# Subtracting the softmax maxima of four attention units on TensorE, and placing three pieces of work elsewhere, in a windowed attention followed by a SoLU block

## The chip, the core and the metric

The kernel runs on one core of a Trainium2 chip. The metric is the device time of one execution in microseconds. Before the change it is 503.84 us, the median of three runs (502.17 to 504.85). The core has five engines with a sequencer each: TensorE (PE in the profile, with its weight loads as PEld), VectorE (DVE), ScalarE (ACT), GpSimd (POOL) and SyncE (SP), which here issues the DMA transfers. They run side by side and wait for one another by semaphores. Matmuls write to PSUM, which this kernel sees as eight banks of 512 fp32 columns (`banks[:, 0:8]`).

## What is computed

Attention over 8 batches, 8 heads, 576 positions and 64 dimensions, in which a position sees only the 32 before it (heads 0 to 3) or every fourth of the 128 before it (heads 4 to 7). Its output, 4608 tokens of 512, goes through a block with the SoLU activation and a layer norm:

```python
scores = scale * np.matmul(q, k.transpose(0, 1, 3, 2))
scores = np.where(masks[None, :, :, :], scores, -1000000000.0)
scores = scores - np.max(scores, axis=-1, keepdims=True)
attn = np.exp(scores)
attn = attn / (np.sum(attn, axis=-1, keepdims=True) + 1e-09)
attn_out = np.matmul(attn, v)
...
h = x @ w_in                                   # 4608 x 512 by 512 x 1024
sm = e / (np.sum(e, axis=-1, keepdims=True) + 1e-09)   # e = exp(h - max)
solu = h * sm
ln = (solu - mu) / np.sqrt(var + 1e-06) * g_ln
out = ln @ w_out                               # 1024 x 512
```

## The kernel before

**Units.** A unit is two heads of one batch; there are 32. For unit n, SyncE loads queries and keys (`qN`) and values (`vN`). TensorE computes the scores of a unit (`SN`, function `scores`): two bf16 matmuls write the mask into PSUM (L244, an identity times the mask), and 80 small fp32 matmuls add the scores (L252; `order` prints x40 for a shape, the trace counts each fp32 matmul twice, as it does its weight load). The result is 128 partitions by 2 x 5 x 64: for every query 64 keys. Then come `maxN` (VectorE, L278, maximum over 64 keys, ten per partition), `subN` (the maximum is subtracted), `expN` (ScalarE, L295), `sumN` and `invN` (VectorE, L299 to L304), `normN` (GpSimd, L309), `turnN` (a transpose on VectorE, L314) and `VN` (TensorE, probabilities by values, L330). `xhN` and `xlN` split the output into two fp32r parts, which are the columns of x.

For units 0 to 9 the mask is written by TensorE, and `subN` is a VectorE operation from PSUM to SBUF (L288); for units 2, 5 and 6 ScalarE copies the scores first (`cpN`) and GpSimd subtracts (L291).

**PSUM.** `ps_s(n)` gives the scores of units 0 to 4 the banks 2 and 3, and all later units a part of banks 6 and 7. The output of `VN` has banks of its own (`ps_x`). The block's first product of even and odd tiles lies in pairs of banks too: hc1 of the opening, the second half of tile 1, starts in a pair that the scores used.

**The block.** 36 tiles of 128 tokens. `haI`, `hbI`, `hcI`, `hdI` are the four quarters of the first product (L398, 6 matmuls each, fp32r by three terms: hi x hi, hi x lo, lo x hi), then `peakI` (VectorE, L409), `eI` (ScalarE), `gateI` and `midI` (VectorE, L433, L441), `varI` (GpSimd), `forthI` and `backI` (the tile goes out to a scratch array in DRAM and comes back with the 1024 features in another order), `trAI`, `trBI` (VectorE transposes, L505), `thAI` to `tlBI` (split in hi and lo), and `oI`, the second product (L528, 24 matmuls: for each of eight groups of 128 features hi x hi, hi x lo, lo x hi), `outI`.

**Weights.** They come as 64-bit floats in 16 pieces (`wB`, 0 to 7 of w_in, 8 to 15 of w_out) and are turned to fp32 by bit operations: `absB`, `lowB` (ScalarE, L805, L815), `clampB`, `signB`, `joinB` (VectorE, L821, L828, L836), `gainB` and `hiB` (ScalarE), `loB` (GpSimd, and for some pieces, 13 among them, VectorE, L850). A product waits for the pieces that it reads: group f of `oI` for piece 8 + f.

**What sets the order.** Nothing is scheduled: each engine runs its instructions in the order in which the program issues them. For the first units and tiles that order is a list of words, `OPENING`, run from left to right; after it `STEP` and `PAIR` repeat for the rest, unchanged here. So a word moved in the list is moved on each engine that it has instructions on, SyncE's queue of DMA issues among them.

Of the kernel before, what the change touches and what calls it, by code (L numbers as in the profile page):

```python
# [9 lines left out]
F32 = mybir.dt.float32  # L10
# [4 lines left out]
AF = mybir.ActivationFunctionType  # L15
# [8 lines left out]
P = 128  # L24
# [4 lines left out]
WQ = 2 * WIN  # L29
NG = P // WIN  # L30
GQ = S // NG
NS = -(-GQ // WIN)
# [15 lines left out]
F64_MAX = REBIAS * float(np.array(0x47EFFFFF, np.uint32).view(np.float32))  # L48
FIRST = 6
OPENING = (  # L50
# [25 lines left out]
)  # L76
STEP = (
    (
# [45 lines left out]
OFFSET = {'qt2': 48, 'kt2': 32, 'vt2': 48, 'qt3': 48, 'kt3': 48, 'vt3': 48}  # L124
SLOTS = "t0 t1 t2 t3 raw4 raw5 tp t0 t1 t2 t3 raw4 raw5 tp t3 tp".split()
MERGED = 5
SHIFT = {}


@with_exitstack  # L130
def windowed_attention_then_solu_kernel(
# [10 lines left out]
    nc = tc.nc  # L142
# [6 lines left out]
    const = ctx.enter_context(tc.tile_pool(name="const", bufs=1))  # L149
    units = ctx.enter_context(tc.tile_pool(name="units", bufs=3))  # L150
    att = ctx.enter_context(tc.tile_pool(name="att", bufs=1))
# [9 lines left out]
    id_bf = packed[:, 0 : P // 2].bitcast(BF16)  # L161
    mask_sb = packed[:, P // 2 : P // 2 + NS * WQ].bitcast(BF16).rearrange("p (d c) -> p d c", d=2)
    g_sb = packed[:, P // 2 + NS * WQ :]
    mhalf = const.tile([P, 1], F32, name="mhalf")
    below = const.tile([P, 1], F32, name="below")
    w_i = const.tile([P, KT, 2, 2, 512], F32R, name="w_i")
# [3 lines left out]
    banks = psum.tile([P, 8, 512], F32, name="banks")  # L170
# [10 lines left out]

    def ps_s(n):
        if n < MERGED:
            return banks[:, 2:4, 0 : NS * WQ]
        return banks[:, 6:8, GQ : GQ + NS * WQ]

    nc.vector.memset(mhalf, -0.5)
# [45 lines left out]
    st = {}  # L233

    def scores(n):

        qt, kt = loaded[n]["q"], loaded[n]["k"]
        dil = int(n % NPAIR >= NPAIR // 2)
        ps = ps_s(n)
        st[n] = {"ps": ps.rearrange("p h (s w) -> p h s w", w=WQ)}  # L240
        on_pe = n in PE_MASK
        if on_pe:
            for h in range(2):
                nc.tensor.matmul(  # L244
                    out=ps[:, h, :], lhsT=id_bf, rhs=mask_sb[:, dil, :],
                    start=True, stop=False, skip_group_check=True,
                )
        for i in range(NS):
            for h in range(2):
                for c in range(NG):  # L250
                    q0 = GQ * c + WIN * i
                    nc.tensor.matmul(  # L252
                        out=ps[WIN * c : WIN * c + WIN, h, WQ * i : WQ * i + WQ],
                        lhsT=qt[D * h : D * h + D, q0 : q0 + WIN],
                        rhs=kt[D * h : D * h + D, q0 : q0 + WQ],
                        start=not on_pe,
                        stop=True,
                        skip_group_check=True,
                    )

    def soft_mask(n):
        if n in PE_MASK:
            return
        dil = int(n % NPAIR >= NPAIR // 2)
        sm = st[n]["sm"] = att.tile([P, 2, NS, WQ], F32, name=f"sm{n % 2}")
        nc.vector.tensor_tensor(  # L266
            out=sm.rearrange("p h s w -> p h (s w)"), in0=ps_s(n),
            in1=mask_sb[:, dil, :].unsqueeze(1).broadcast_to([P, 2, NS * WQ]),
            op=ALU.add,
        )  # L270

    def wide(x):
        return x.unsqueeze(3).broadcast_to([P, 2, NS, WQ])
# [9 lines left out]

    def soft_sub(n):
        mx = st[n]["mx"]
        if n in PE_MASK and n not in ACT_SCORES:
            sm = st[n]["sm"] = att.tile([P, 2, NS, WQ], F32, name=f"sm{n % 2}")
            nc.vector.tensor_tensor(out=sm, in0=st[n]["ps"], in1=wide(mx), op=ALU.subtract)  # L288
            return
        eng = nc.gpsimd if POOL_SUB else nc.vector  # L290
        eng.tensor_tensor(out=st[n]["sm"], in0=st[n]["sm"], in1=wide(mx), op=ALU.subtract)  # L291

    def soft_exp(n):
        sm = st[n]["sm"]
        nc.scalar.activation(out=sm, in_=sm, func=AF.Exp, scale=0.125)  # L295

# [174 lines left out]
    def part_of_t(name, i):  # L471
        name = f"{name}{i % TH_BUFS}"
        if name in SHIFT and name not in shifted:
            shifted.add(name)
            moe.tile([P, SHIFT[name]], F32, name=f"before_{name}", bufs=1)
        return moe.tile([P, FT, P], F32R, name=name, bufs=1)
# [371 lines left out]
    def conv_lo(b):  # L848
# [5 lines left out]

    one = {
        "q": load_qk, "v": load_v, "w": load_w,
        "pack": lambda _: nc.sync.dma_start(out=packed, in_=pack),
        "abs": conv_abs, "low": conv_low, "clamp": conv_clamp, "sign": conv_sign,
        "join": conv_join, "gain": conv_gain, "hi": conv_hi, "lo": conv_lo,
        "S": scores, "mask": soft_mask, "max": soft_max, "cp": soft_copy, "sub": soft_sub, "exp": soft_exp,  # L860
        "sum": soft_sum, "inv": soft_inv, "norm": soft_norm, "turn": turn,
        "V": attend, "xc": x_copy, "xh": spread_hi, "xl": spread_lo,
# [47 lines left out]
    for word in OPENING.split():  # L910
        name = word.rstrip("0123456789")
# [86 lines left out]
```

## Time and profile before

| | |
|---|---|
| median of three runs | 503.84 us |
| the profiled execution | 503.07 us, span 501.3 us |
| TensorE busy | 471.7 us, 94% of the span |
| VectorE, ScalarE, GpSimd busy | 351.9, 289.1, 295.7 us |
| DMA | 94.07 MB, mean 188 GB/s |
| subtraction of a unit on VectorE (L288) | 0.82 us |
| subtraction of a unit on GpSimd (L291) | 1.26 us |

The page cuts the span into 40 slices of 12.5 us and gives the busy share of each engine in tenths. In a timeline row stand the start, the length, the engine, the line, the operation with output and inputs by their names, how many instructions were joined in the row, and in brackets how long the engine had been idle and what released it. "issue" stands for a wait that nothing in the profile explains. In the view by stretches each row is a stretch of time with the busy time and count of TensorE, weight loads, VectorE, ScalarE and GpSimd, then the granted TensorE clock (1.00 is full), the DMA share and GB/s.

### The profile page before, as it was taken

The numbers are of one execution on the slowest core, as the hardware profiler recorded it, in microseconds if no ns is written. First come the engines' busy times: TensorE is split into PE (matmuls) and PEld (weight loads), VectorE is DVE, ScalarE is ACT, GpSimd is POOL, SyncE is SP. The second block draws the span as 40 slices with busy tenths as digits, with TensorE's granted clock in tenths as the row PEclk, the third lists the DMA queues.
The fourth block names the chain that finished last, engine by engine and source line by source line (L and its number), as shares of the span: only waits on it lengthen the run. The fifth ranks groups of instructions, "written<-read, shape, count | busy, mean of one in ns | idle before, by whom it ended". The sixth has DMA issues, their size and how long they took to land.

```text
span 501.3 us, 16598 instructions
## 1 busy us (share of the span) xinstructions
PE 471.7 (94%) x7088; PEld 379.3 (76%) x7088; DVE 351.9 (70%) x619; ACT 289.1 (58%) x481; POOL 295.7 (59%) x367
## 2 busy tenths in 40 slices
PE   3449988999999999999999999999999999999997
PEld 2337766888887888878778787878787888888876
DVE  3998897768446788787868686868676864445562
ACT  3756986645233445444457575757575767666552
POOL 0463774575344665778976666665757555766440
PEclk9999997999999999999999999999999999999999
DMA  8999637554347555565667677776765545454461
GB/s 283 349 377 346 190 78 252 150 177 154 112 130 226 179 174 162 171 194 169 200 170 221 199 218 205 214 209 211 212 211 164 161 129 147 104 157 141 109 181 70
DMA packets 50905, 94.07 MB, mean 188 GB/s; under 512 B 5648, under 2 KB 25616, under 8 KB 50832
## 3 DMA queue, kind: packets, MB, share of 16 engines
q1 hardware_dynamic: 49968, 92.30, 59.8%
q8 instruction: 55, 0.90, 0.7%
q10 hardware_dynamic: 864, 0.72, 0.4%
q14 instruction: 18, 0.15, 0.1%
HBM read 59.97 MB, written 28.31 MB: 176 GB/s over the span
## 4 chain that ended last, share of the span: by engine, by line
PE 87%; DVE 8%; DMA 2%; issue 2%; ACT 1%; SPq 0%; DVEq 0%; ACTq 0%
PE banks L528 37%; PE banks L758 20%; PE banks L398 17%; PE banks L330 6%; PE banks L252 6%; DMA t<-w_in 1%; PE banks L549 1%; DVE mag L821 1%; DVE mag L836 1%; DVE t L433 1%; DVE mx L278 1%; DVE rs L299 1%; DVE low L828 1%; DMA mid<-t 1%; PE banks L244 0%
## 5 line engine op out<-in xcount | busy, mean ns | idle before, releaser
L528 PE MATMUL banks<-w_o,th 128*128 128x512 f32 x560 | 174.9, 393 | 0.0
L528 PEld LDWEIGHTS banks<-w_o,th 128*128 128x128 f32 x560 | 103.6, 188 | 21.8 <-ACT th L513 0.4
L519 POOL TENSOR_TENSOR tl<-t,th 128x512 fp32r<-128x512 f32 x68 | 88.1, 1310 | 48.4 <-ACT th L513 48.1
L528 PE MATMUL banks<-w_o,tl 128*128 128x512 f32 x280 | 109.3, 390 | 0.0
L398 PE MATMUL banks<-w_i,x_hi 128*128 128x512 f32 x256 | 84.0, 410 | 0.1
L528 PEld LDWEIGHTS banks<-w_o,tl 128*128 128x128 f32 x280 | 52.5, 188 | 11.6 <-DVE tl L519 0.4
L513 ACT CAST th<-t 128x512 fp32r<-128x512 f32 x72 | 43.5, 620 | 28.3 <-DVE t L505 14.6
L398 PEld LDWEIGHTS banks<-w_i,x_hi 128*128 128x128 f32 x256 | 48.3, 195 | 11.1 <-DVE mu L433 0.2
L505 DVE STREAM_TRANSPOSE t<-raw 128x512 f32<-128x512 f32 x72 | 47.4, 687 | 10.4 <-DMA raw<-mid 10.3
L398 PE MATMUL banks<-w_i,x_lo 128*128 128x512 f32 x128 | 51.3, 401 | 0.0
L330 PEld LDWEIGHTS banks<-pt,vt 32*64 32x64 f32 x2816 | 35.2, 137 | 20.9 <-issue 10.5
L449 ACT ACTIVATE e<-t 128x1024 f32<-128x1024 f32 x35 | 37.0, 1057 | 21.4 <-DVE t L445 21.0
L330 PE MATMUL banks<-pt,vt 32*64 32x64 f32 (+3 forms) x2816 | 38.7, 234 | 9.9 <-DMA vt<-vw 4.0
L291 POOL TENSOR_TENSOR sm<-sm,mx 128x640 f32<-128x640 f32 x25 | 31.6, 1263 | 24.2 <-DVE mx L278 17.0
L266 DVE TENSOR_TENSOR sm<-banks,packed 128x640 f32<-128x640 f32 x22 | 18.1, 823 | 38.8 <-PE banks L252 38.8
L295 ACT ACTIVATE sm<-sm 128x640 f32<-128x640 f32 x32 | 23.6, 738 | 35.0 <-POOL sm L291 32.4
L252 PEld LDWEIGHTS banks<-kt,qt 64*32 64x32 f32 x2560 | 29.9, 113 | 16.1 <-issue 9.8
L540 ACT ACTIVATE ob<-banks,rstd 128x512 f32<-128x512 f32 x35 | 24.0, 686 | 27.9 <-issue 16.7
L252 PE MATMUL banks<-kt,qt 64*32 64x64 f32 x2560 | 35.7, 241 | 4.0 <-DMA qt<-qT 3.2
L782 DVE CUSTOM_DVE_ANT_0 t<-banks,t 128x512 f32<-128x512 f32 x30 | 20.7, 690 | 22.4 <-PE banks L758 17.0
L776 ACT COPY t<-banks 128x512 f32<-128x512 f32 x30 | 17.6, 588 | 30.3 <-PE banks L758 30.3
L442 ACT ACTIVATE t<-t,mu 128x1024 f32<-128x1024 f32 x23 | 26.4, 1149 | 11.0 <-DVE mu L441 11.0
(156 smaller groups left out, 880.0 us busy)
## 6 DMA issues: line engine op xcount, KB each, us to landing
mid<-t SPq DMA_DIRECT2D x140, 128.0 KB, 2.4
raw<-mid SPq DMA_DIRECT2D x34, 512.0 KB, 3.8
vt<-vw SPq DMA_DIRECT2D x32, 384.0 KB, 3.9
kt<-kT SPq DMA_DIRECT2D x32, 312.0 KB, 4.0
qt<-qT SPq DMA_DIRECT2D x32, 296.0 KB, 4.3
out<-ob SPq DMA_DIRECT2D x35, 256.0 KB, 2.6
x_hi<-x SPq DMA_DIRECT2D x12, 288.0 KB, 3.6
t<-w_in SPq DMA_DIRECT2D x5, 512.0 KB, 8.4
```

The costliest lines, as they stand in the source:

```text
L252: nc.tensor.matmul(out=ps[WIN * c : WIN * c + WIN, h, WQ * i : WQ * i + WQ], lhsT=qt[D * h : D * h + D, q0 : q0 + WIN], rhs=kt[D * h : D * ...
L291: eng.tensor_tensor(out=st[n]["sm"], in0=st[n]["sm"], in1=wide(mx), op=ALU.subtract)
L330: nc.tensor.matmul(out=ps_x[D * h : D * h + D, c, c0 : c0 + k1 - k0], lhsT=vt[WIN * c : WIN * c + WIN, i, D * h : D * h + D], rhs=pt[WIN * ...
L398: nc.tensor.matmul(out=ps_h(i)[:, half], lhsT=a[:, kt, xs], rhs=w_i[:, kt, half, part, :], start=(kt == 0 and k == 0), stop=(kt == KT - 1 ...
L442: nc.scalar.activation(out=dst, in_=src, func=AF.Identity, bias=mu, scale=1.0)
L449: nc.scalar.activation(out=e, in_=t, func=AF.Square, accum_out=per_tile(i, "sq"))
L505: nc.vector.transpose(out=turned(i)[:, cut(c)].rearrange("p k (a r) -> p k a r", r=WIN), in_=ms[i]["mv"].rearrange("p (a k s) -> p k a s", ...
L513: nc.scalar.copy(out=ms[i]["th"][:, cut(c)], in_=turned(i)[:, cut(c)])
L519: eng.tensor_tensor(out=ms[i]["tl"][:, cut(c)], in0=turned(i)[:, cut(c)], in1=ms[i]["th"][:, cut(c)].bitcast(F32), op=ALU.subtract,)
L528: nc.tensor.matmul(out=ps_o(i), lhsT=a[:, f, :], rhs=w_o[:, f, part, :], start=(f == 0 and k == 0), stop=(f == FT - 1 and k == 2), skip_gr ...
L540: nc.scalar.activation(out=ob, in_=ps_o(i), func=AF.Copy, scale=rstd)
L758: nc.tensor.matmul(out=banks[:, bank], lhsT=left(pa, kt), rhs=right(pb, kt), start=j in (1, 2, 5) and kt == 0 and k == 0, stop=kt == 1 and ...
```

## The change

Four things, all in the opening.

1. **Subtraction on TensorE for units 0, 1, 3 and 4** (`PE_SUB`). A new word `neg` makes a negated fp32 identity `minus` (128 x 128) on ScalarE. `soft_sub` issues two fp32 matmuls of 320 columns instead of the VectorE operation: `minus` times the maxima, broadcast over the 64 keys, is added to the scores where they lie in PSUM. `soft_exp` of these units reads PSUM and writes SBUF.
2. **PSUM of units 0 to 4.** Even units stay in banks 2 and 3, odd units go to banks 0 and 1.
3. **Values of unit 1.** `v1` is issued ahead of three weight loads rather than behind them.
4. **Unit 8.** `S8` goes from behind hb4, next to S9, to between V6 and V7; `max8` and `sub8`, still on VectorE, go from behind the transposes of tile 0 to behind `mid3`.

```diff
 OPENING = (
-    "pack q0 S0 w0 q1 max0 sub0 low0 abs0 w3 exp0 abs3 S1 q2 clamp0 low3 sign0 sum0 w2 inv0 "
+    "pack q0 S0 neg w0 q1 max0 sub0 low0 abs0 w3 exp0 abs3 S1 q2 clamp0 low3 sign0 sum0 w2 inv0 "
...
-    "norm1 turn0 S2 max2 low2 cp2 clamp1 sign2 V0 q3 turn1 sub2 clamp2 abs4 sign1 w10 hi3 low4 "
-    "w9 exp2 low7 join2 w5 join1 v1 xh0 clamp4 sign4 hi1 S3 w6 lo1 abs5 low5 sum2 inv2 xl0 max3 "
+    "norm1 turn0 S2 max2 low2 cp2 clamp1 sign2 V0 q3 turn1 sub2 clamp2 abs4 sign1 v1 w10 hi3 "
+    "low4 w9 exp2 low7 join2 w5 join1 xh0 clamp4 sign4 hi1 S3 w6 lo1 abs5 low5 sum2 inv2 xl0 "
...
+PE_SUB = (0, 1, 3, 4)
...
+    minus = const.tile([P, P], F32, name="minus")
...
         if n < MERGED:
-            return banks[:, 2:4, 0 : NS * WQ]
+            b = n % 2 * 2
+            return banks[:, 2 - b : 4 - b, 0 : NS * WQ]
         return banks[:, 6:8, GQ : GQ + NS * WQ]
...
     def soft_sub(n):
         mx = st[n]["mx"]
+        if n in PE_SUB:
+            for h in range(2):
+                nc.tensor.matmul(
+                    out=ps_s(n)[:, h, :],
+                    lhsT=minus,
+                    rhs=mx[:, h, :].unsqueeze(2).broadcast_to([P, NS, WQ]),
+                    start=False, stop=True, skip_group_check=True,
+                )
+            return
...
     def soft_exp(n):
+        if n in PE_SUB:
+            sm = st[n]["sm"] = att.tile([P, 2, NS, WQ], F32, name=f"sm{n % 2}")
+            nc.scalar.activation(out=sm, in_=st[n]["ps"], func=AF.Exp, scale=0.125)
+            return
...
+        "neg": lambda _: nc.scalar.activation(out=minus, in_=id_bf, func=AF.Copy, scale=-1.0),
```

How the instructions stand on the engines, at three places. On TensorE, around unit 4 and the first product of the block; before (L252 scores of unit 4, L330 values of unit 2, L398 first product):

```order
L252 MATMUL banks<-kt_499,qt_498 32x64 x40
L330 MATMUL banks<-pt_510,vt_489 64x64 x24
L330 MATMUL banks<-pt_510,vt_489 64x48 x8
L330 MATMUL banks<-pt_510,vt_489 64x16 x8
L398 MATMUL banks<-w_i,x_hi 128x512 x2
L398 MATMUL banks<-w_i,x_lo 128x512
```

and now, where the lines are 3 to 16 higher (L255, L346, L414) and L291 is the subtraction of unit 4:

```order
L255 MATMUL banks<-kt_503,qt_502 32x64 x40
L346 MATMUL banks<-pt_515,vt_493 64x64 x24
L346 MATMUL banks<-pt_515,vt_493 64x48 x8
L346 MATMUL banks<-pt_515,vt_493 64x16 x8
L414 MATMUL banks<-w_i,x_hi 128x512 x2
L414 MATMUL banks<-w_i,x_lo 128x512
L414 MATMUL banks<-w_i,x_hi 128x512 x2
L414 MATMUL banks<-w_i,x_lo 128x512
L291 MATMUL banks<-mx,minus 128x320 x2
```

The subtraction of unit 4 stands behind the six matmuls of ha0, ahead of hc1. That of unit 3 stands further up, between V1 and the masks of unit 4.

On TensorE, further on, values of units 6 and 7 now (they stood next to one another before):

```order
L346 MATMUL banks<-pt_1167,vt_739 64x64 x24
L346 MATMUL banks<-pt_1167,vt_739 64x48 x8
L346 MATMUL banks<-pt_1167,vt_739 64x16 x8
L247 LDWEIGHTS packed
L247 MATMUL banks<-packed 128x320
L247 LDWEIGHTS packed
L247 MATMUL banks<-packed 128x320
L255 MATMUL banks<-kt_742,qt_741 32x64 x40
L346 MATMUL banks<-pt_1181,vt_745 64x64 x24
```

The mask and scores of unit 8 (L247, L255) came in between.

On VectorE, at the same place, now (L449 gate3, L457 mid3, L281 and L300 maximum and subtraction of unit 8, L852 join11, L521 trA0, L401 xl7):

```order
L449 ISA t_1283,mu<-banks,e 128x1024
L449 ISA mu 128x1
L837 TENSOR_SCALAR mag_749<-mag_749 128x512
L457 TENSOR_SCALAR mu<-mu 128x1
L281 TENSOR_REDUCE mx<-banks 128x10
L300 TENSOR_TENSOR sm_1335<-banks,mx 128x640
L852 SCALAR_TENSOR_TENSOR mag_749<-mag_749,low_758 128x512
L521 STREAM_TRANSPOSE t_890<-raw_1165 128x512
L837 TENSOR_SCALAR mag_1327<-mag_1327 128x512
L401 TENSOR_TENSOR x_lo<-banks,x_hi 128x576
```

Before, the two operations of unit 8 stood behind the maximum of tile 4 (L409, peak4) and ahead of gate4:

```order
L409 TENSOR_REDUCE nmax<-banks 128x1
L278 TENSOR_REDUCE mx<-banks 128x10
L288 TENSOR_TENSOR sm_1400<-banks,mx 128x640
L433 ISA t_1405,mu<-banks,e 128x1024
L433 ISA mu 128x1
```

So nine operations of VectorE, from join11 to peak4, are now behind them, xl7 and the last sign of the weights among them.

42 rows, old and new, of the table OPENING are left out of this document.

## The prediction

> **What bounds the kernel now.** I read the page first, for the slices and the clock, then busy time by stage, then the timeline of single engines where TensorE waits.
>
> ```profile
> span 501.3 us, 16598 instructions
> ...
> PE 471.7 (94%) x7088; PEld 379.3 (76%) x7088; DVE 351.9 (70%) x619; ACT 289.1 (58%) x481; POOL 295.7 (59%) x367
> ...
> PE   3449988999999999999999999999999999999997
> ...
> DVE  3998897768446788787868686868676864445562
> ```
>
> ```profile
> 0.00:38.30 38.30, 16.25 (x683) 12.04 (x683) 29.46 (x51) 20.78 (x33) 14.59 (x15) 1.00 0.94 337
> 38.30:95.00 56.70, 52.79 (x1000) 41.48 (x998) 46.91 (x80) 44.72 (x72) 33.28 (x44) 0.94 0.66 212
> 95.00:250.00 155.00, 154.84 (x2343) 124.75 (x2342) 114.20 (x175) 68.36 (x116) 98.84 (x133) 1.00 0.55 168
> 250.00:480.00 230.00, 230.00 (x2974) 186.39 (x2973) 152.96 (x303) 148.12 (x248) 144.46 (x170) 1.00 0.60 176
> ```
>
> The columns of the second view are the stretch, its length, the busy time of TensorE, its weight loads, VectorE, ScalarE and GpSimd, the granted clock, the DMA share and GB/s. From 95 to 480 us TensorE is busy without a gap (154.84 of 155, 230.00 of 230). So whatever TensorE gains or loses ahead of 95 us moves the end by the same amount. Until 38.3 us it is busy for only 16.25 us; VectorE has 29.46 and the DMA engines a share of 0.94. The stage between, to 95 us, loses 3.9 us in waits and more to a clock of 0.94.
>
> **The opening: the subtraction on TensorE.** These rows, of VectorE, ScalarE and TensorE, carry the first part.
>
> ```profile
> 7.52 0.82 DVE L278 TENSOR_REDUCE mx<-banks 128x10 f32<-128x640 f32 x1 [6.61 <-PE banks L252]
> 8.38 0.82 DVE L288 TENSOR_TENSOR sm<-banks,mx 128x640 f32<-128x640 f32 x1
> ...
> 14.05 0.81 DVE L278 TENSOR_REDUCE mx<-banks 128x10 f32<-128x640 f32 x1
> ...
> 16.12 0.69 DVE L836 SCALAR_TENSOR_TENSOR mag<-mag,low 128x512 int32<-128x512 int32 x1
> 16.73 0.81 DVE L299 TENSOR_REDUCE rs<-sm 128x10 f32<-128x640 f32 x1
> ```
>
> ```profile
> 8.89 0.76 ACT L815 ACTIVATE low<-t,below 128x512 int32<-128x512 uint16 x1 [6.67 <-DMA t<-w_in]
> ...
> 10.11 0.72 ACT L295 ACTIVATE sm<-sm 128x640 f32<-128x640 f32 x1
> ...
> 15.75 0.74 ACT L295 ACTIVATE sm<-sm 128x640 f32<-128x640 f32 x1 [0.58 <-DVE sm L288]
> ```
>
> ```profile
> 20.76 0.71 PE L244 MATMUL banks<-packed 128*128 128x320 bf16 x2
> 21.97 0.42 PE L252 MATMUL banks<-kt,qt 64*32 64x64 f32 x5 [0.50 <-DMA qt<-qT]
> 23.18 1.35 PE L252 MATMUL banks<-kt,qt 64*32 64x64 f32 x75 [0.78 <-issue]
> 27.18 1.15 PE L330 MATMUL banks<-pt,vt 32*64 32x32 f32 x52 [2.65 <-DMA vt<-vw]
> 30.07 0.95 PE L330 MATMUL banks<-pt,vt 32*64 32x64 f32 x44 [1.74 <-issue]
> ...
> 33.11 1.41 PE L252 MATMUL banks<-kt,qt 64*32 64x64 f32 x80
> 34.45 0.36 PE L330 MATMUL banks<-pt,vt 32*64 32x64 f32 x1
> 36.87 1.46 PE L330 MATMUL banks<-pt,vt 32*64 32x64 f32 x79 [2.06 <-issue]
> 38.26 1.22 PE L398 MATMUL banks<-w_i,x_hi 128*128 128x512 f32 x2
> ...
> 40.72 0.62 PE L398 MATMUL banks<-w_i,x_hi 128*128 128x512 f32 x2
> ```
>
> *Price of one subtraction.* Removed are four VectorE operations of 0.82 us, 3.3 us in all. Added are four pairs of fp32 matmuls with 320 columns, which no row of before has. Below, the pair of masks is the same shape in bf16: 0.71 us (20.76). Above, the scores stream 320 fp32 columns in each place of the array in 1.41 us (33.11), and the two halves of the new form, each over the whole array, may not overlap: 2 x 1.41 = 2.8 us. I take 2.4 us, nearer the upper row because that row has the operand type; once the clock is up the scores take 1.04 us (81.70, below), so there I take 1.3.
>
> *The negated identity* is one ScalarE operation, at most the 0.76 us of the row at 8.89, and ScalarE idles ahead of that row for 6.67 us; it costs nothing unless it is late for 8.4 us, when the first subtraction reads it.
>
> *Units 0 and 1.* Subtraction 0 runs from 8.4 to 10.8 instead of 9.2. exp starts at 10.9 rather than 10.11, so the sum behind it comes 0.9 late, and with VectorE's order fixed the maximum of unit 1 ends at 15.75 rather than 14.86. Subtraction 1 then ends at 18.2 and its exp at 19.05, where the sum started at 16.73. VectorE has only a sign and a join (0.45 + 0.69) to put there and then idles: from here it is 2.4 us late, and the saved 0.82 is used up. Unit 2's scores stand behind subtraction 1 on TensorE, so they are late by about the same, 2.2 us.
>
> *Instruction fetch.* The three waits called "issue" at 23.18, 30.07 and 36.87 end 6.9 and 6.8 us apart. Counting weight load and matmul as a pair, 75 + 52 or 44 + 2 + 80 + 1 = 127 pairs lie between two of them, near 256 instructions; and 2 x 7088 instructions over the 55 packets of
>
> ```profile
> q8 instruction: 55, 0.90, 0.7%
> ```
>
> are 258 each, of 16 KB. So TensorE pauses at block edges while the DMA engines are full, and the last edge sets when V2, and behind it the first product of the weights, starts (36.87). The edges are a chain: each block is asked for when one is done. Each subtraction adds 8 instructions ahead of them, so the edges slide back into V0's end, V1 and the end of S4, and the chain, starting 2.2 us later, ends near 39.1. V2 runs after it: its start 34.45 to 36.87 becomes 39.4, and ha0's 38.3 becomes 40.9, **2.6 us late**. The skill's page "Runtime: NRT & Kernel Launch", under "Instruction fetch mechanics", says the queue fetches ahead and that crossing a block is mostly hidden; here three crossings show 0.78, 1.74 and 2.06 us, so the trace disagrees in this stage, and its own case is rival two.
>
> *Unit 4.* On TensorE its subtraction stands behind six products of ha0, and hc1 behind it waits for exp 4, since both use the same pair of PSUM banks. ha0's six take 2.5 us in before (38.26 to 40.72), so the subtraction runs from 43.3 to 44.6, exp takes 0.74, and hc1 starts at 45.5 instead of 40.72: **4.8 us late**, 2.2 of it new. Behind hc1 queues all of TensorE's work. With subtractions at 0.7/0.45 the same walk gives 1.9; if in addition the crossings cost nothing, VectorE's saving comes through ahead of V2 and it gives -0.8; at 2.8 it gives 5.6.
>
> *Values of unit 1 ahead of three weight loads*: V1 waited 2.65 us for its values until 27.18. It would start near 25.6, but the block edge inside V1 sets its end, so I count nothing. If that cover were gone it would be worth up to 1.6 us to V1 alone.
>
> **The stage around unit 8.**
>
> ```profile
> 71.12:74.53 3.41, 1.48 (x82) 1.34 (x83) 3.41 (x8) 3.41 (x7) 2.92 (x7) 1.00 0.58 132
> 74.54:77.95 3.41, 3.41 (x10) 2.64 (x9) 3.20 (x7) 3.41 (x7) 2.43 (x6) 0.50 1.00 293
> ...
> 81.37:84.77 3.40, 1.63 (x85) 1.13 (x84) 3.19 (x4) 1.99 (x4) 1.09 (x1) 1.00 0.61 208
> 84.78:88.18 3.40, 3.40 (x87) 2.72 (x86) 3.37 (x8) 2.56 (x5) 0.00 (x0) 0.50 0.80 251
> ```
>
> ```profile
> 72.95 1.08 PE L330 MATMUL banks<-pt,vt 32*64 32x64 f32 x80 [1.99 <-DVE x_lo L385]
> ...
> 81.70 1.04 PE L252 MATMUL banks<-kt,qt 64*32 64x64 f32 x80
> 84.51 0.47 PE L244 MATMUL banks<-packed 128*128 128x320 bf16 x2 [1.77 <-DVE sm L288]
> ...
> 92.71 0.62 PE L528 MATMUL banks<-w_o,th 128*128 128x512 f32 x2
> ...
> 96.11 0.62 PE L528 MATMUL banks<-w_o,th 128*128 128x512 f32 x2
> ```
>
> ```profile
> 78.25 0.44 DVE L828 TENSOR_SCALAR low<-tp 128x512 uint16<-128x512 uint16 x1
> ...
> 93.28 0.71 DVE L505 STREAM_TRANSPOSE t<-raw 128x512 f32<-128x512 f32 x1 [2.65 <-DMA raw<-mid]
> 93.92 0.79 DVE L288 TENSOR_TENSOR sm<-banks,mx 128x640 f32<-128x640 f32 x1
> 94.62 1.36 DVE L850 TENSOR_TENSOR w_o<-mag,w_o 128x512 fp32r<-128x512 f32 x1
> ```
>
> Times here are those of before; the lag of the opening comes on top. Each stretch of 3.4 us in which TensorE was busy for less than half (1.48, 1.63) is followed by one of 3.4 us at half clock, which loses half of it, 1.7 us. S8 (masks and scores, 0.4 + 1.0 = 1.4 us) moves into the 1.99 us for which V7 waits, so it leaves its old place (-1.4) and fills the first idle stretch (-1.7). S9 waited 1.77 us because the subtraction of unit 8 stood late on VectorE; it is long done then (-1.8), and the second idle stretch goes too (-1.7). Maximum and subtraction 8 (0.82 each) now stand ahead of xl7 and cost the last products of tile 4 about 0.4. Sum: -6.2, so tile 0's output product would start at 86.5 instead of 92.71.
>
> But its sixth group, 3.4 us in, reads a weight that VectorE finishes at 95.98, behind a transpose that waits until 93.28 for a DMA: in before it starts at 96.11, 0.13 us after. Nothing in the change brings that transfer forward by as much. Its issue follows the work on tile 4, whose products end 1.3 us earlier (1.7 less 0.4), while the last weight load, released by the row at 78.25, is issued 1.4 later since maximum and subtraction 8 stand ahead of it. So the weight comes between 0.3 and 1.6 us earlier; I take 1.0. TensorE waits some 4 us inside the output product, and by the two cases above a half clock of 1.7 us follows. The stage gives -1.0 + 1.7 = **+0.7**; ends are -6.2 (no wait there) and +1.7.
>
> **Sum.** 503.07 us of the profiled execution (span 501.3 and 1.8 around it) + 4.8 + 0.7 = **508.6 us**. The median of the three runs is 503.84, 0.15% above that execution; 0.5% is 2.5 us, about what a measurement of this kernel tells from no change, so "same" is about 500.6 to 505.6.
>
> **Rivals.**
> 1. *Faster: the transfer is early enough.* A subtraction costs as little as the masks (opening +1.9), and the weight and its DMA come with tile 4, so that the wait inside the output product is gone (stage -6.2): 498.8 us. For it: DMA share is 0.61 to 0.80 there, not full. Against: the weight comes 0.13 us ahead of its use already, behind a wait of 2.65 us for DMA. Chance 0.15.
> 2. *Crossings are hidden, or lie elsewhere.* Then V2 follows S4 at 37.3, ha0 is late by 0.5, hc1 starts at 43.3, 2.6 late: 503.07 + 2.6 + 0.7 = 506.4. Against: three equal distances. Chance 0.10. With cheap subtractions alone: 503.07 + 1.9 + 0.7 = 505.7, chance 0.10.
> 3. *Same: half the stage's gain stays.* The opening loses 4.8, and with it the DMA queues gain time on TensorE, so the weight is 3 us early: 503.07 + 4.8 - 3.1 = 504.8. For it: weight loads follow ScalarE and VectorE, not TensorE. Chance 0.15.
> 4. *Slower still: subtraction 4 breaks the warm-up.* TensorE idles for exp 4 just as the clock rises, and a half clock of 1.7 us follows; at 2.8 us a subtraction the opening is 5.6: 503.07 + 5.6 + 1.7 + 0.7 = 511.1. It decides if the wait is over half a stretch of 3.4 us; I expect 0.9. Chance 0.10.
>
> **How the numbers follow.** The forecast, 506.5 to 510, has 0.40. The range 500.0 to 512.5 leaves out rival 1 and the far part of rival 4. Slower: forecast, rival 4 and the first of rival 2, 0.40 + 0.10 + 0.10 and a part of the second, 0.60; faster: rival 1 and a little of 3, 0.16; same: 0.24.
>
> **What would show it.** Subtractions of 0.9 to 1.4 us a matmul before 40 us; VectorE idle ahead of unit 1's sum, released by exp; "issue" waits inside S4 and none ahead of V2; TensorE waiting for exp 4 ahead of hc1; S8 ahead of V7 and no wait ahead of S9; a wait of some 4 us inside the first output product, released by a weight. I am wrong if the subtraction takes under 1 us, if the edges are crossed without a pause, or if the output product runs through without a wait.

## The result, and the profile after

The changed kernel takes 508.31 us (median of 6 runs, 506.07 to 510.5) against 502.67 us (500.1 to 504.85) for the kernel before on the same chips: ratio 1.0117, 95% interval 1.0088 to 1.0147, so 1.2% slower. The forecast was 508.6. The profiled execution took 507.59 us, 4.5 us over that of before. The page of the changed kernel has these lines (among them the 40 slices of TensorE, of VectorE and of the granted clock):

```profile
span 505.7 us, 16632 instructions
...
PE   4568987999999999999999999999999999999997
...
DVE  1899888767637788877868685868686865445562
...
PEclk9769998899999999999999999999999999999999
...
q8 instruction: 55, 0.90, 0.7%
```

TensorE's first slices are fuller (4568 for 3449), VectorE's first two emptier (18 for 39): the subtractions moved. The granted clock changes inside the opening. In before this row is

```profile
PEclk9999997999999999999999999999999999999999
```

Ahead of the first change that a profile records, the clock reads full in these views, but the durations differ: the first subtraction of the changed kernel takes 2.47 us where the clock reads 1.00, the second 2.50 where it reads 0.50. In before a pair of products takes 1.22 us at 38.26 and 0.62 from 40.72, and the pair at 39.71 lies between with 0.94, so half clock lasted until about 40.4 us. The opening on TensorE in the changed kernel, with the price of a subtraction (L291), in the timeline (these rows count each plain fp32 matmul twice: x4 are the two matmuls of a subtraction, x80 the 40, not 80, of a unit's scores):

```profile
6.99 1.39 PE L255 MATMUL banks<-kt,qt 64*32 64x64 f32 x80 [3.11 <-DMA qt<-qT]
9.39 2.47 PE L291 MATMUL banks<-mx,minus 128*128 128x320 f32 x4 [1.01 <-DVE mx L281]
...
16.64 2.50 PE L291 MATMUL banks<-mx,minus 128*128 128x320 f32 x4 [3.04 <-DVE mx L281]
18.94 0.74 PE L247 MATMUL banks<-packed 128*128 128x320 bf16 x2
19.61 1.17 PE L255 MATMUL banks<-kt,qt 64*32 64x64 f32 x80
...
24.02 0.28 PE L346 MATMUL banks<-pt,vt 32*64 32x16 f32 x1 [0.89 <-issue]
...
34.63 0.90 PE L255 MATMUL banks<-kt,qt 64*32 64x64 f32 x69 [0.50 <-DMA qt<-qT]
36.21 0.33 PE L255 MATMUL banks<-kt,qt 64*32 64x64 f32 x11 [0.68 <-issue]
36.47 1.08 PE L346 MATMUL banks<-pt,vt 32*64 32x64 f32 x80
37.48 0.73 PE L414 MATMUL banks<-w_i,x_hi 128*128 128x512 f32 x2
...
38.98 1.24 PE L291 MATMUL banks<-mx,minus 128*128 128x320 f32 x4
41.01 0.73 PE L414 MATMUL banks<-w_i,x_hi 128*128 128x512 f32 x2 [0.79 <-ACT sm L308]
```

and on VectorE the sum of unit 1, which waits for exp:

```profile
19.92 0.82 DVE L315 TENSOR_REDUCE rs<-sm 128x10 f32<-128x640 f32 x1 [1.90 <-ACT sm L308]
```

A subtraction takes 2.47 and 2.50 us, and 1.24 at full clock (2.4 and 1.3 forecast). Unit 4's is 1.24 us with 0.79 of waiting for exp behind it. The sum of unit 1 is 3.2 us later than before; 0.9 of that is that the first queries landed 0.9 us later in this execution (6.99 for 6.09). But the first product of the weights (L414) starts at 37.48, earlier than before's 38.26.

Around unit 8 (TensorE, then ScalarE and VectorE):

```profile
73.33 1.04 PE L255 MATMUL banks<-kt,qt 64*32 64x64 f32 x80
75.88 1.32 PE L346 MATMUL banks<-pt,vt 32*64 32x64 f32 x80 [1.52 <-DVE x_lo L401]
...
85.03 1.04 PE L255 MATMUL banks<-kt,qt 64*32 64x64 f32 x80
88.73 1.22 PE L414 MATMUL banks<-w_i,x_hi 128*128 128x512 f32 x2 [2.67 <-DVE mu L449]
```

```profile
74.40 0.64 ACT L384 CAST x_hi<-banks 128x576 fp32r<-128x576 f32 x1 [1.20 <-PE banks L255]
```

```profile
84.84 1.22 DVE L425 TENSOR_REDUCE nmax<-banks 128x1 f32<-128x1024 f32 x1 [0.56 <-PE banks L414]
87.45 1.22 DVE L449 CUSTOM_DVE_ANT_0 t<-banks,e 128x1024 f32<-128x1024 f32 x1 [1.38 <-ACT e L440]
```

S8 runs at 73.33, ahead of V7, and no wait stands ahead of S9 any more (85.03). Yet V7 waits 1.52 us all the same, since xh6 on ScalarE (74.40) now waits for S8; and the first product of tile 5 waits 2.67 us for gate4 (L449). There is no wait inside the first output product.

### The profile page after: what moved, and what is told of

Read it like the earlier page. It is cut to its first block, busy times and chain, and to the rows that moved or that the text cites. A ratio compares the mean times of both kernels' runs of the same rounds, so it can differ in the third digit from the quotient of the medians.

```text
span 505.7 us, 16632 instructions
## 1 busy us (share of the span) xinstructions
PE 477.3 (94%) x7104; PEld 381.3 (75%) x7104; DVE 351.2 (69%) x615; ACT 289.2 (57%) x482; POOL 294.9 (58%) x367
## 4 chain that ended last, share of the span: by engine, by line
PE 90%; DMA 3%; DVE 3%; issue 2%; ACT 1%; SPq 0%; DVEq 0%; ACTq 0%
PE banks L544 36%; PE banks L774 20%; PE banks L414 19%; PE banks L346 6%; PE banks L255 6%; DMA qt<-qT 3%; PE banks L291 1%; PE banks L565 1%; DVE t L449 1%; DMA mid<-t 1%; ACT e L440 0%; DVE mx L281 0%; ACT sm L308 0%; PE banks L247 0%; DVE rs L315 0%
## 5 line engine op out<-in xcount | busy, mean ns | idle before, releaser
L414 PE MATMUL banks<-w_i,x_hi 128*128 128x512 f32 x256 | 83.9, 409 | 4.2 <-DVE mu L449 2.9
L414 PEld LDWEIGHTS banks<-w_i,x_hi 128*128 128x128 f32 x256 | 48.0, 194 | 15.1 <-DVE mu L449 3.2
L521 DVE STREAM_TRANSPOSE t<-raw 128x512 f32<-128x512 f32 x72 | 47.3, 687 | 10.3 <-DMA raw<-mid 10.3
L414 PE MATMUL banks<-w_i,x_lo 128*128 128x512 f32 x128 | 51.2, 400 | 0.0
L346 PEld LDWEIGHTS banks<-pt,vt 32*64 32x64 f32 x2816 | 34.0, 133 | 17.8 <-issue 7.5
L346 PE MATMUL banks<-pt,vt 32*64 32x64 f32 (+3 forms) x2816 | 37.4, 229 | 7.1 <-DVE x_lo L401 5.0
L255 PEld LDWEIGHTS banks<-kt,qt 64*32 64x32 f32 x2560 | 29.1, 109 | 18.2 <-issue 14.2
L255 PE MATMUL banks<-kt,qt 64*32 64x64 f32 x2560 | 34.9, 233 | 6.3 <-DMA qt<-qT 3.6
L311 ACT ACTIVATE sm<-sm 128x640 f32<-128x640 f32 x28 | 20.7, 738 | 32.8 <-POOL sm L303 32.2
L440 ACT ACTIVATE e<-t,nmax 128x1024 f32<-128x1024 f32 x19 | 21.9, 1152 | 20.3 <-DVE nmax L805 19.6
```

The costliest lines, as they stand in the source:

```text
L255: nc.tensor.matmul(out=ps[WIN * c : WIN * c + WIN, h, WQ * i : WQ * i + WQ], lhsT=qt[D * h : D * h + D, q0 : q0 + WIN], rhs=kt[D * h : D * ...
L346: nc.tensor.matmul(out=ps_x[D * h : D * h + D, c, c0 : c0 + k1 - k0], lhsT=vt[WIN * c : WIN * c + WIN, i, D * h : D * h + D], rhs=pt[WIN * ...
L414: nc.tensor.matmul(out=ps_h(i)[:, half], lhsT=a[:, kt, xs], rhs=w_i[:, kt, half, part, :], start=(kt == 0 and k == 0), stop=(kt == KT - 1 ...
L440: nc.scalar.activation(out=e, in_=h, func=AF.Exp, bias=nmax, scale=1.0, accum_out=se)
L521: nc.vector.transpose(out=turned(i)[:, cut(c)].rearrange("p k (a r) -> p k a r", r=WIN), in_=ms[i]["mv"].rearrange("p (a k s) -> p k a s", ...
```

## The experiments

All were timed in five rounds beside the kernel before, whose median was 502.6 to 503.4 us in these sets.

**Only the subtractions** (subs_only): the changed kernel with every word at its place of before, apart from `neg`.

```diff
-    "... sign1 v1 w10 hi3 low4 w9 exp2 low7 join2 w5 join1 xh0 ..."
+    "... sign1 w10 hi3 low4 w9 exp2 low7 join2 w5 join1 v1 xh0 ..."
-    "... V6 S8 var2 xh6 ... mid3 max8 sub8 xh7 ... hi11 trB0 ... v11 tlB0 ..."
+    "... V6 var2 xh6 ... mid3 xh7 ... hi11 S8 trB0 ... v11 max8 sub8 tlB0 ..."
```

> Only the four subtractions on TensorE (with the negated identity and the two pairs of banks); values of unit 1 and unit 8 stay where they were. Theory A (the subtractions and the 32 instructions that they put into TensorE's stream cost the time): 505.5 to 508 us, ratio 1.006 to 1.011, with a wait of 0.7 to 0.9 us for exp ahead of hc1 and waits called issue of 0.4 to 1.3 us behind 45 us, where before has none; around unit 8 the wait of 1.8 us ahead of S9 and two half-clock stretches stay. Theory B (the places of unit 8 cost it): within 0.3% of before, about 502 to 504 us.

Measured: 506.53 us, ratio 1.0075 (1.0047 to 1.0104). Theory A holds for the larger part. The waits called issue stand where it said, at 51.1 and 57.0 us (0.59, 0.45), but that the slid block edges make them does not follow: place8 and halves0 (below), with no instruction added on TensorE ahead of them, pause for 1.21 and 1.27 us at 49.2 and 48.2. No run changes the banks of the odd units or the negated identity alone; every kernel with subtractions on TensorE has both, so their share is not separated.

**Only unit 8** (unit8_only): the kernel before with `S8` between V6 and V7, `max8 sub8` behind `mid3`.

```diff
-    "... V6 var2 xh6 ... mid3 xh7 ... hi11 S8 trB0 ... v11 max8 sub8 tlB0 ..."
+    "... V6 S8 var2 xh6 ... mid3 max8 sub8 xh7 ... hi11 trB0 ... v11 tlB0 ..."
```

> Only unit 8 is moved. Theory A: 503.0 to 504.5 us, at most 0.35% over before: the wait ahead of S9 goes, S8 runs ahead of V7, but V7 still waits and the first product of tile 5 waits 2 to 3 us for gate4, so about 1 us is lost up to the first output product. Theory B: 505 us or more. If the stage had given what a moved S8 and a gone wait are worth by themselves: 498 to 500 us.

Measured: 505.67 us, ratio 1.0048 (1.0021 to 1.0075), more than theory A said and in the range of theory B, though the waits are those that theory A named. TensorE and ScalarE in its timeline:

```profile
73.47 1.23 PE L330 MATMUL banks<-pt,vt 32*64 32x64 f32 x80 [1.52 <-DVE x_lo L385]
...
86.04 0.74 PE L398 MATMUL banks<-w_i,x_hi 128*128 128x512 f32 x2 [2.68 <-DVE mu L433]
```

```profile
71.98 0.64 ACT L368 CAST x_hi<-banks 128x576 fp32r<-128x576 f32 x1 [1.25 <-PE banks L252]
```

The three waits of the changed kernel are there without any subtraction on TensorE, to 0.05 us. So they belong to unit 8's place.

**S8 behind xh6 in the program** (xh6_first).

```diff
-    "... xl5 V6 S8 var2 xh6 e3 ..."
+    "... xl5 V6 var2 xh6 S8 e3 ..."
```

> The changed kernel with the word S8 behind xh6, so that every engine's order is as in the changed kernel, and only what xh6 waits for can differ. If xh6 waits for S8 only because it is issued behind it: xh6 starts within 0.2 us of the end of V6 rather than 1.4 us later, V7's wait falls from 1.5 us to under 0.7, tile 4's chain comes 1 to 1.4 us earlier and the time is 506.0 to 507.3 us (ratio to before 1.007 to 1.009). If xh6 waits for something that S8 holds anyway: no change, 508 us (1.010 to 1.013).

Measured: 507.09 us, ratio 1.0072 (1.0040 to 1.0104); against the changed kernel's 1.0117 the intervals overlap. The time lies in the first range. xh6 starts at 73.79, right behind V6, as expected, but V7 still waits, 0.92 us, and S8 waits too:

```profile
72.67 1.08 PE L346 MATMUL banks<-pt,vt 32*64 32x64 f32 x80
74.48 0.43 PE L247 MATMUL banks<-packed 128*128 128x320 bf16 x2 [0.73 <-ACT x_hi L384]
74.84 1.04 PE L255 MATMUL banks<-kt,qt 64*32 64x64 f32 x80
76.80 1.08 PE L346 MATMUL banks<-pt,vt 32*64 32x64 f32 x80 [0.92 <-DVE x_lo L401]
```

Whichever is written first, the other waits: the output of V6 (`ps_x`, banks 4 to 7) and the scores of unit 8 (banks 6 and 7) share two banks, in different columns. That the shared banks are the reason is not shown, as no run parts them. From the start of V6 to V7 it is 4.13 us here and 3.94 in the changed kernel, against 3.07 before (72.95 - 69.88). So S8 does not fit into V7's wait; about 1 us of it comes on top.

**32 more instructions on TensorE** (phase32): 16 bf16 matmuls ahead of S0, whose results are overwritten.

```diff
-    "pack q0 S0 w0 ..."
+    "pack q0 pad S0 w0 ..."
+    def pad():
+        for _ in range(16):
+            nc.tensor.matmul(
+                out=ps_s(0)[:, 0, 0:WQ], lhsT=id_bf, rhs=mask_sb[:, 0, 0:WQ],
+                start=True, stop=True, skip_group_check=True,
+            )
```

> The kernel before with 16 small bf16 matmuls ahead of S0, where TensorE waits 2 us for the queries: 32 more instructions in its stream and nothing else; their result is overwritten. If the places of the block edges matter: the waits called issue stand at other places than in before (inside V0 and S4, and one or two behind 45 us), and the time is 503.5 to 506 us. If they do not: 502 to 503.5 us, within 0.2% of before.

Measured: 503.99 us, ratio 1.0023 (0.9993 to 1.0054): it can't be told from no change, and not from a loss of half a per cent either. The waits called issue did stand elsewhere, inside V0 and S4 (1.83 and 0.31 us), but none behind 45 us. Its profile, though, shows the clock. It has the same waits ahead of V7 and S9 as before (1.95 and 1.77 us), but no half clock behind them. The clock changes on lines 3.41 us apart (the half clocks, below). Counted back from this profile's one drop, at 498.36 us behind the last matmul, two of these lines lie at 71.70 and 81.94, inside the two waits (70.90 to 72.85 and 81.02 to 82.79). Cut there, no stretch is busy for less than half (last three columns: clock, DMA share, GB/s):

```profile
68.28:71.69 3.41, 2.62 (x87) 1.95 (x86) 3.38 (x7) 2.96 (x5) 3.05 (x4) 1.00 0.32 65
71.70:75.10 3.40, 2.16 (x85) 1.88 (x86) 3.40 (x8) 3.40 (x6) 2.90 (x7) 1.00 0.63 176
75.11:78.51 3.40, 3.40 (x17) 2.81 (x16) 3.16 (x7) 3.37 (x7) 2.31 (x7) 1.00 0.95 293
78.52:81.93 3.41, 2.50 (x88) 1.79 (x87) 2.15 (x4) 1.89 (x3) 3.41 (x4) 1.00 0.83 234
81.94:85.34 3.40, 2.55 (x87) 2.02 (x87) 3.37 (x6) 2.81 (x6) 0.40 (x1) 1.00 0.75 252
```

Before lost 3.4 us to half clock behind the same waits. From the start of V6 to the first output product it is 19.9 us here (69.82 to 89.71) and 22.8 in before (69.88 to 92.71), so two such stretches cost 2.9 us.

**Unit 4 alone, and units 0, 1 and 3 alone** (sub4_only, subs013): subs_only with

```diff
-PE_SUB = (0, 1, 3, 4)
+PE_SUB = (4,)          # sub4_only
+PE_SUB = (0, 1, 3)     # subs013
```

> Only unit 4 is subtracted on TensorE, units 0, 1 and 3 on VectorE as before; identity and banks as changed, all places as before. If the subtraction that stands in the first product, with the wait for exp behind it, carries the cost (1.24 + 0.79 = 2.0 us where TensorE has no slack): 504.2 to 505.5 us, ratio 1.003 to 1.006, and hc1 starts 2 us later against ha0 than in before. If units 0, 1 and 3 carry it: 502.3 to 503.3 us, under 1.002.

> Units 0, 1 and 3 on TensorE, unit 4 on VectorE. If the opening is held by DMA and hides them: 502.3 to 503.5 us (ratio under 1.002), ha0 starts no later than in before. If they make the opening longer by the later sums on VectorE: 504 to 506 us (1.003 to 1.007), ha0 1.5 to 3 us later.

Measured: 505.64 us, ratio 1.0048 (1.0017 to 1.0079), and 504.80 us, ratio 1.0053 (1.0024 to 1.0082). Each carries about half a per cent, the two together 0.75 rather than 1.0, though the intervals don't rule 1.0 out. In sub4_only hc1 starts 5.85 us behind ha0 (38.25 to 44.10), 3.4 later than in before and not 2, as its first products still ran at half clock. In subs013 the first product starts at 37.85, no later than before and at full clock, and V3 behind it has to wait:

```profile
36.84 1.08 PE L346 MATMUL banks<-pt,vt 32*64 32x64 f32 x80
37.85 0.73 PE L414 MATMUL banks<-w_i,x_hi 128*128 128x512 f32 x2
...
43.65 1.08 PE L346 MATMUL banks<-pt,vt 32*64 32x64 f32 x80 [1.43 <-DVE pt L330]
```

```profile
42.76 0.83 DVE L330 STREAM_TRANSPOSE pt<-sm 128x640 f32<-128x640 f32 x1
```

The transpose of unit 3 runs at 42.76, where before has it at 40.44: the 2.3 us that VectorE lost at the sum of unit 1 are still there. The wait takes back what the full clock had gained (V3 starts at 43.56 in before), and a pause called issue of 1.15 us at 49.80 follows. With unit 4 also on TensorE, 1.24 + 0.79 us ahead of V3 cover the same lag: no wait stands ahead of V3 in the changed kernel.

**Unit 8 placed in VectorE's idle time** (place8).

```diff
-    "... V6 var2 xh6 e3 ... hi11 S8 trB0 sign13 peak4 ... v11 max8 sub8 tlB0 ..."
+    "... V6 var2 xh6 S8 e3 ... hi11 trB0 sign13 max8 sub8 peak4 ... v11 tlB0 ..."
```

> The kernel before with unit 8 placed otherwise: S8 between V6 and V7 but behind xh6 in the program, maximum and subtraction behind the last sign and ahead of the maximum of tile 4, where VectorE idles. If the first product of tile 5 waits for gate4 anyway (maximum, exp and gate of tile 4, some 4 us behind its product): gate4 comes 1.6 us earlier and the time falls by 0.5 to 1.5 us, 501.3 to 502.3 us (0.997 to 0.999). If the wait ahead of S9 and S8 itself were the cost: 498.5 to 500 us (0.992 to 0.995). If moving S8 costs in itself: 504 us or more.

Measured: 503.25 us, ratio 1.0011 (0.9987 to 1.0034): nothing gained, none of the three as written. What gate4 gains, V7 gives back: 4.15 us from V6 to V7 (70.66 to 74.81) against 3.07. And the first output product now waits 1.01 us, at 96.18, for weight 13 (VectorE, L850).

**Half an output product in the wait for gate4** (halves0; in halves_late13 `lo13` stays behind `thA1`). As place8, and

```diff
-    "... back1 q12 sign15 ha5 ... tlB1 o0 turn8 ..."
+    "... back1 q12 sign15 oA0 ha5 ... tlB1 oB0 turn8 ..."
-    "... hi13 trB2 lo12 sub9 thA1 lo13 lo15 ..."
+    "... hi13 lo12 lo13 trB2 sub9 thA1 lo15 ..."
```

> As place8, and the first half of tile 0's second product (groups 0 to 3) stands ahead of tile 5's first product, in the wait for gate4; the last half stays, and on VectorE the low part of weight 13 goes ahead of the transpose that waits for a DMA. If the hole ahead of gate4 is the lever: 2 to 4 us less than before, 498.5 to 501 us (0.991 to 0.996). If weights 12 and 13 hold the second half: a wait of 1 to 3 us inside it, and no more than place8 gives.

> As halves0, but the low part of weight 13 stays on VectorE behind the transpose that waits for a DMA. If that weight is what bounds tile 0's output product, as the prediction had it: TensorE waits 3 to 5 us inside the second half of that product, released by VectorE's weight, and the time is 502.5 to 505 us, 1.2 to 3 us over halves0 (501.3). If gate4 alone was the bound: no such wait, 501 to 502 us.

Measured: halves0 501.30 us, ratio 0.9971 (0.9945 to 0.9997), the only kernel here whose interval lies below 1, and just so; halves_late13 503.26 us, ratio 1.0002 (0.9970 to 1.0035). In halves0 the groups 0 to 3 fill the hole and the product of tile 5 follows without a wait:

```profile
81.35 1.04 PE L252 MATMUL banks<-kt,qt 64*32 64x64 f32 x80
82.32 0.73 PE L528 MATMUL banks<-w_o,th 128*128 128x512 f32 x2
...
85.19 0.62 PE L398 MATMUL banks<-w_i,x_hi 128*128 128x512 f32 x2
...
92.05 0.50 PE L528 MATMUL banks<-w_o,th 128*128 128x512 f32 x1 [0.85 <-POOL w_o L850]
```

With weight 13 late, TensorE waits three times inside the second half, 0.16 us at 94.23 and the two below, the last time for VectorE:

```profile
95.58 0.50 PE L528 MATMUL banks<-w_o,th 128*128 128x512 f32 x1 [0.85 <-POOL w_o L850]
...
97.36 0.50 PE L528 MATMUL banks<-w_o,th 128*128 128x512 f32 x1 [0.83 <-DVE w_o L850]
```

So weight 13 is a bound, as the prediction had it, but of 0.83 us, not of the 3 to 5 expected. It binds in place8 (1.01 us) and in subs013 (0.83 at 97.05) as well; in the changed kernel it does not.

**Values of unit 1 alone, and with halves0; the subtractions on top** (v1_only, halves_v1, halves_v1_subs).

```diff
-    "... sign1 w10 hi3 low4 w9 exp2 low7 join2 w5 join1 v1 xh0 ..."
+    "... sign1 v1 w10 hi3 low4 w9 exp2 low7 join2 w5 join1 xh0 ..."
```

> Only the values of unit 1 go ahead of three weight loads. If V1, which waits 2 to 5 us for them in the kernels without this move, is what holds the opening: 500 to 501.8 us (0.995 to 0.998). If the weight loads that come later, or the sums on VectorE, hold the first product anyway: within 0.2% of before, 501.7 to 503.7 us.

> halves0 with the values of unit 1 early: no subtraction on TensorE. If both gains hold: 499.5 to 501 us (0.993 to 0.997). If the values of unit 1 bring nothing: 501 to 502 us.

> The same with the four subtractions on TensorE: beside halves_v1 it is their price in a kernel without the other losses. If they cost by themselves (late sums in the opening, 1.24 + 0.79 us inside the first product): 2 to 4 us over halves_v1, 502 to 504.5 us. If they cost only together with before's or the change's placing of unit 8: under 1 us over halves_v1.

Measured: 502.68 us, ratio 0.9986 (0.9962 to 1.0011); 502.60 us, 0.9979 (0.9954 to 1.0004); 505.25 us, 1.0042 (1.0018 to 1.0066). Early values give nothing that can be measured. The second lies above both ranges expected of it, so the gain of halves0 is not confirmed. The subtractions cost 2.65 us between the last two, as expected, and 3.7 in subs_only, within the intervals: a price of their own, not one of the places.

## Why the prediction was right, and where its steps were wrong

The time was met within 0.3 us, but by luck: two terms were off, in opposite directions (4.8 us for 2.8, 0.7 for 2.4). The starts of V6 in the profiles measure the first term, free of what comes later (us from the start of the span, each the first record of V6 in that profile, one profile to a kernel):

| kernels | start of V6 | mean |
|---|---|---|
| no subtraction on TensorE: before, phase32, v1_only, unit8_only, place8, halves0, halves_late13, halves_v1 | 69.88, 69.82, 68.38, 69.52, 70.66, 69.59, 69.53, 71.06 | 69.80 |
| all four: subs_only, xh6_first, the changed kernel, halves_v1_subs | 73.38, 72.67, 71.94, 72.45 | 72.61 |
| unit 4 alone; units 0, 1 and 3 alone | 73.57; 71.36 | |

- **The price of a subtraction** was right: 2.47 to 2.50 us for 2.4, 1.24 for 1.3.
- **Units 0 and 1** were right: VectorE idles 1.90 us ahead of the sum of unit 1 and is 2.3 us late from there (3.2 less the 0.9 of the queries), 2.4 forecast. Where it comes to bear was wrong: not at V2, but at V3 (the wait of 1.43 us in subs013).
- **Instruction fetch was the step that failed.** "The chain, starting 2.2 us later, ends near 39.1" and ha0 is "2.6 us late": the edges did slide into V0's end and the end of S4 (24.02, 36.21), and there is no wait ahead of V2. But the last edge came at 36.21, not 39.1; before had 36.87, and V2 starts in time. So the edges are not a chain that later work pushes back by as much. That they are edges holds: the pauses stand 127 or 128 pairs of weight load and matmul apart, or whole multiples of that (892 for 7 in halves_v1, 4079 for 32 in the changed kernel). But the one ahead of V2 took 2.06 us in before, 0.39 in unit8_only and nothing in halves0, with the same instructions on TensorE up to there. Where it shows a pause, the last of these edges lies between 36.1 and 38.4 us in the profiles with units 0, 1 and 3 on TensorE, and between 35.3 and 36.9 in the others. What sets its time was not settled. Nor are the crossings hidden, as rival two had it: pauses of 0.2 to 2.3 us stand at two or more such edges in every one of these profiles. The page "Runtime: NRT & Kernel Launch" of the Trainium skill ("Instruction fetch mechanics") calls them mostly hidden, and here, too, the traces disagree for the opening.
- **Unit 4** was half right. Subtraction and exp take 2.03 us out of TensorE's path (2.2 forecast); but the six products ahead run in 1.5 us, not 2.5, because the clock was full from 33.7 us. In the 3.41 us before that, with the subtraction of unit 3, TensorE was busy throughout:

```profile
30.32:33.72 3.40, 3.40 (x85) 2.39 (x70) 3.40 (x5) 1.79 (x4) 2.34 (x2) 0.50 1.04 411
```

  The subtractions are not the only way there: in halves_late13, without any, the pair at 36.56 takes 0.73 us, where no pause stands ahead of V2. So hc1 starts at 41.01 instead of 45.5. **The opening's term was 4.8 us; it measured 2.8** (72.61 - 69.80 at V6). At V3 the same two groups start at 42.88 and 44.86 on average, 2.0 us apart; most of the rest is pauses called issue between 45 us and V6, 0.45 and 1.04 us on average.
- **Unit 8** was mis-sized the other way, +0.7 for 2.4 us (unit8_only, 1.1 to 3.8), and its mechanism was another. That S8's 1.4 us, S9's 1.8 and the half clocks go, and a late weight takes them back, is not what happened: the first output product ran through without a wait, which the prediction had named as a sign that it is wrong. (Its own rows give that wait 5.2 us, from 86.5 + 3.4 to 95.1, not some 4, and the 1.6 us as an upper end for the weight is not worked out.) S9's wait had been standing in front of another: the product of tile 5 needs gate4. In the kernel before, gate4 on VectorE and that product on TensorE have these rows:

```profile
84.37 1.22 DVE L433 CUSTOM_DVE_ANT_0 t<-banks,e 128x1024 f32<-128x1024 f32 x1
```

```profile
86.24 1.22 PE L398 MATMUL banks<-w_i,x_hi 128*128 128x512 f32 x2
```

  Gate4 ends at 85.59, 0.65 us ahead of the product, so no more than that was to be gained there. Taking S9's wait out leaves the hole: 2.67 us at 88.73. And S8 adds to V7's wait rather than filling it. From the start of V6 to the first output product it is 23.8 us in the changed kernel and 22.8 in before, with two half-clock stretches in both; with one each 22.1 in unit8_only and 21.1 in subs013. So the place costs 1.0 us by itself. The rest of the 2.4 is within its interval, and was not traced.
- **The half clocks** did follow the rule taken from two cases, "Each stretch of 3.4 us in which TensorE was busy for less than half" is followed by one at half clock, once the stretches are cut where the clock changes. Within each profile the changes lie whole steps of 3.41 us apart: 74.54 and 84.78 in before, 33.72, 78.10 and 88.34 in the changed kernel, 72.76 and 499.42 in v1_only, 125 steps. In the 13 profiles that show a change, 259 stretches between these lines begin at full clock from 45 to 118 us. All 11 with TensorE busy for less than half were followed by half clock, none of the 243 with 0.58 or more, and four of the five between (0.51 to 0.56). Full clock came back behind stretches busy for 0.89 or more, not behind those up to 0.83. So the same wait costs a half clock or nothing, by where it falls: one that lies across a line, as both do in phase32, leaves both sides busier. This is a count over profiles; no run moved the lines. In the changed kernel the two stretches that hold most of the waits for V7 and gate4 were busy for 1.90 and 1.13 us:

```profile
74.69:78.09 3.40, 1.90 (x83) 1.58 (x84) 2.67 (x6) 3.40 (x7) 2.65 (x10) 1.00 0.63 127
78.10:81.50 3.40, 3.40 (x10) 2.63 (x9) 3.37 (x6) 2.97 (x5) 0.22 (x2) 0.50 0.99 356
84.93:88.33 3.40, 1.13 (x82) 0.88 (x80) 2.02 (x2) 2.23 (x4) 1.69 (x2) 1.00 0.86 272
88.34:91.75 3.41, 3.02 (x7) 2.44 (x8) 3.34 (x9) 2.73 (x6) 0.00 (x0) 0.50 0.78 202
```

  So what failed was not this rule but the waits: V7's stayed, and gate4's took the place of S9's. The page "TensorE: Matmul & The Clock Gate" of the Trainium skill (Part 1, on the clock gate) has a free-running window of 3413 ns, and says that results vary with its phase; both agree with these steps and with phase32.
- **Early values of unit 1** were right at nothing (0.9986, interval over 1).
- **Rivals.** One (faster) and three (same) fell: the stage around unit 8 gave nothing back. The cheap subtraction of rivals one and two did not come. (The 0.60 for slower leaves out the second part of rival two, of which it says that it takes a share.) The warm-up of rival four did not break: the clock stays full from 33.72 to 78.10.
- **Behind the first output product** the prediction has TensorE busy without a gap. Of the 4.5 us between the two profiled executions, 2.1 lie ahead of V6, 1.0 from there to the first output product, and 1.5 behind it, most of that in one more pause; no other profile here has one over 0.4 us there:

```profile
312.68 0.32 PE L255 MATMUL banks<-kt,qt 64*32 64x64 f32 x8 [1.21 <-issue]
```

The parts, each measured alone, add up to 0.75 + 0.48 - 0.14 = 1.09%, beside 1.17% for the whole.

## What to carry to other kernels

Moving an operation from a full engine to an idle one pays only if the chain through it is not made longer: here VectorE saved 0.82 us a unit, and the next step of the same unit came 2.3 us later, with nothing to fill the gap. Before a wait is taken out, look for what the instructions behind it wait for next: here the next input was ready only 0.65 us ahead of its use, and taking 1.8 us out left a hole of 2.7. The only gain seen came from work put into that hole (half an output product, 0.3%, at the edge of what can be measured). Scores and output that lie in the same PSUM banks made TensorE and ScalarE wait for one another here, though their columns differ.

## What the runs showed of the hardware that was not expected

- Two fp32 matmuls of 128 x 128 by 320 columns take 2.47 to 2.50 us at half clock and 1.24 at full clock; as many bf16 matmuls take 0.71 and 0.44.
- The clock can be full inside the opening: in the changed kernel it is granted from 33.7 us; in before, by the durations of the products, from about 40.4.
- One kernel's executions spread over 6 us (before: 499.8 to 506.3 over all sets). Two things in the profiles vary and can add up to as much: the number of half-clock stretches between 60 and 110 us (none to three, about 1.5 us each) and the pauses at block edges, which come up to 2.3 us long at one edge and not at all at the same edge in another kernel.
